# Moving weight decodes between the stages of a fused attention and two-mixer kernel

## The chip, the core and the metric

One core of a Trainium2 chip runs the whole program. The metric is the device time of one execution in microseconds (us); lower is better. The kernel before has a median of 1039.64 us over three runs (1037.52 to 1042.57). Engines: TensorE (PE in the profile; PEld is its weight load), VectorE (DVE), ScalarE (ACT), GpSimd (POOL) and the DMA queue of SyncE (SP).

## What is computed

```python
# q, k, v: 4 x 8 heads x 576 tokens x 64, float32; w_phi: 64 x 128
phi(x): proj = x @ w_phi;  proj -= max(|proj|);  concat(exp(proj), exp(-proj))
kv  = phi(k)^T @ v;  z = sum over tokens of phi(k)
x   = (phi(q) @ kv) / (phi(q) . z + 1e-6)          # then 4 x 576 x 512
u   = x + (x^T @ U @ V)^T                           # first mixer, rank 32
x   = u + relu(u @ w_ch1) @ w_ch2                   # 512 -> 2048 -> 512
u   = x + (relu(x^T @ w_tok1) @ w_tok2)^T           # second mixer, 576 -> 256 -> 576
out = u + relu(u @ w_ch1') @ w_ch2'                 # 512 -> 1536 -> 512
```

## The kernel before

**Number format.** The weights of the mixers arrive as float64. `decode64` (lines 161 to 176) turns a block of 128 x 512 of them into float32: two ACT conversions, `w` from the upper words (L166) and `r` from the lower words (L167), then two DVE bit operations, `r_` (L169) and `w_` (L172). Nearly every matmul is done in pieces: a number is split into a high part (a cast, L102 on ACT or L104 on DVE) and a low part (source minus high part, L107, on POOL or DVE), and three products replace one. `load_half` decodes and splits one **half**: of a tile of 128 hidden units, half 0 holds the first-layer weights (512 x 128) and half 1 the second-layer weights. Names follow: `w_a`, `wh_a`, `wl_a` are the decoded, high and low halves of stage A; `_b` and `_c` are stages B and C. The stage pool has two buffers for the raw words, two for `w`, two for `r`.

**Stage A.** The attention runs in rounds, five to each of 16 head pairs; `at(r, fn)` puts work into round r. In each round one `proj` makes features on PE (`pp`), takes the absolute maximum on DVE (`km`, L310) and subtracts it (`kd`, L107); `k1`, `k2`, `k3`, `q1`, `q2` exponentiate on ACT and multiply on PE (`kvp`, `dT`, `kvt`, `nm`). From the seventh head pair on (`NF32 = 6`), the features are split too (`keh`, `kel`, `qeh`, `qel`, KL), on ACT, DVE and POOL. The first mixer's channel layer has 16 hidden tiles; the first six (`NA`) are computed within the rounds, batch by batch (`ma_u`, `ma_h` for the hidden tile, `ma_y` for the second layer). `M_AT` starts this for batch 0 at round 37. The table `AT_WA` tells in which rounds the twelve halves of these six tiles are decoded (six first layers, then six second layers), and each is fetched `L_WA = 2` rounds before. High parts of first layers are cast on ACT, those of second layers on DVE, low parts are made on POOL.

**The end of stage A.** While batch 3 is computed, each `ma_h` calls `half_next`, which finishes the half that was decoded before (`parts`, `put_half`) and decodes the next one of the ten remaining tiles, which form five pairs. Four pairs have a place in SBUF (`wp`); the fifth gets one only when the attention's memory is given back. `AB.close()` ends the stage.

**Stages B and C.** `channel` computes a chunk of tokens: for each pair p of hidden tiles, `one(p)` (short chunks) or `seven(p)` (long chunks, seven products in place of eight) makes the hidden values (`hpb`, `hhb`, `hlb`), and `second` of the pair before adds to `yb`. Stage B has chunks of 256, 256, 512, 512, 512, 256 tokens, numbered 0 to 5. After each pair the chunk calls its **hooks**, lists of functions. From chunk 3 on, each chunk also carries the token mixing of one batch (`tokmix2`: `x2p`, `hhx`, `gp`, `m2p`) at its tail, and the last one is in chunk 0 of stage C. Weights of stage C have 24 halves. Those of pairs 0, 1, 2 and 5 are decoded by hooks of stage B (`decode`) and stored as float32 in DRAM (`wD`), fetched back late (`fetch_c`) and split (`weights_c`). Pairs 3 and 4 (`DIRECT`) are decoded and split in place (`direct`): one group of two halves in B chunk 5, three in C chunk 0.

**Order of the work.** A scheduler places each engine's instructions in one queue when the program is built, from the order of the code and its own estimates; on the chip each queue runs in that order. `tc.issue_after` keeps an instruction behind a given one.

```python
def ma_h(b, ch, f):                                  # L546
    a, v = relu_split(hp[:, :N], hh, hl)
    if b == B - 1:
        with tc.issue_after(a), tc.issue_after(v):
            for _ in range(2 if f == 0 else 1):
                half_next()
```

Of the kernel before, what the change touches and what calls it, by code (L numbers as in the profile page):

```python
# [8 lines left out]
F32 = mybir.dt.float32  # L9
# [10 lines left out]
P = 128  # L20
# [5 lines left out]
C = 512  # L26
# [7 lines left out]
NB = (NF1 - NA) // 2  # L34
NCP = NF2 // 2
# [60 lines left out]
def body(ctx, tc, kq, vd, w_phi, U, V, wm1, wt1, wt2, wm2, out):  # L96
    nc = tc.nc
# [41 lines left out]
    wD = [dr.tile([P, 2 * C], F32, name=f"wD{f}") for f in range(NF2)]  # L139
# [5 lines left out]
    stage = ctx.enter_context(tc.tile_pool(name="stage", bufs=RAWB))  # L145
# [52 lines left out]
    def h_tile(pool, w, uh, ul, name, tag="m"):  # L198
        hp = pool.tile([P, 512], F32, tag=tag, name=f"hp_{name}")
        wh, wl = w  # L200
        g = []
        for c in range(NC):
            g += [(w1(wh, c), uh[:, c, :]), (w1(wh, c), ul[:, c, :]), (w1(wl, c), uh[:, c, :])]
        group(hp[:, : uh.shape[2]], g)
        return hp

    def relu_split(hp, hh, hl):
        a = nc.scalar.activation(hh, hp, AF.Relu)  # L208
        v = nc.vector.scalar_tensor_tensor(out=hl, in0=hp, scalar=0.0, in1=f32(hh), op0=ALU.max, op1=ALU.subtract)  # L209
        return a.ins, v.ins  # L210
# [15 lines left out]
    wp = psm.tile([P, 512], F32, tag="m", name="wp")  # L226
# [43 lines left out]
    def at(r, fn, *args):  # L270
        rounds.setdefault(r, []).append((fn, args))
# [275 lines left out]
    def ma_h(b, ch, f):  # L547
        nm = f"a{b}_{ch}_{f}"
        hp = h_tile(psm, wA[f], *uhl[b, ch], nm)
        hh, hl = h_pair(f, nm)  # L550
        a, v = relu_split(hp[:, :N], hh, hl)
        if f < NA - 1 or b == B - 2:
            gates[:] = a, v
        hss[b, ch].append((hh, hl))
        if f == 3 and b < B - 2:
            ma_v(b, ch)
        if b == B - 1:
            with tc.issue_after(a), tc.issue_after(v):
                for _ in range(2 if f == 0 else 1):
                    half_next()  # L560

    def ma_s(b, ch, f):
        if f == 0:
# [130 lines left out]
    wp = {}  # L694
# [25 lines left out]
    def parts():  # L720
        while later:
            put_half(*later.pop(0))

    def half_next():
        parts()
        if not halves or halves[0][0] not in wp:
            return
        p, k, i = halves.pop(0)
        if p not in wB:
            wB[p] = pair_tiles(p, "b")  # L730
        later.append((firsts.pop(0) if firsts else take(), wB[p], k, i, "p"))
# [4 lines left out]
    for r in sorted(rounds):  # L736
        if r > end + 7:
            for fn, args in rounds[r]:
                fn(*args)
    while halves and halves[0][0] in wp:  # L740
        half_next()
    parts()
    PS.close()
    AB.close()
    psh = ctx.enter_context(tc.tile_pool(name="psh", bufs=2, space=PSUM, reuse_waits="tile"))
# [2 lines left out]
    pt = ctx.enter_context(tc.tile_pool(name="pt", **right))  # L748
# [2 lines left out]
    TX = ExitStack()  # L751
    tx = TX.enter_context(tc.tile_pool(name="tx", **right))

    words = [(f, k) for p in range(NCP) if p not in DIRECT for k in range(2) for f in (2 * p, 2 * p + 1)]

    def word(f, k):
        return wm2[f][:, k * C : (k + 1) * C], C, f"c{f}_{k}"
# [1 line left out]
    t1s = [(wt1[:, t], 256, f"t1_{t}") for t in range(NT)]  # L759
    t2s = [(wt2[:, j, k * N : (k + 1) * N], N, f"t2_{j}_{k}") for j in range(2) for k in range(2)]  # L760
    ts, ws = t1s + t2s, [word(*x) for x in words]
    stream += ts[:8] + ws[:1] + ts[8:] + ws[1:] + [word(2 * p + i, k) for p in DIRECT for k in range(2) for i in range(2)]

    def decode():
        f, k = words.pop(0)
# [2 lines left out]
    wC = {}  # L768
# [261 lines left out]
    def sums_b(p):  # L1030
        return lambda: sums(p, wB[p])

    def sums_c(p):
        return lambda: sums(p, wC[p])

    ahead = {}

    def fetch_c(p):
        ts = [stage.tile([P, 512], F32, tag=t, name=f"w_c{p}{n}", bufs=2) for n, t in enumerate("wwrr" * (p == 1))]
        for t in (3, 4) * (p != 1):  # L1040
            w = pt.tile([P, 2 * C], F32, tag=f"t{t}", name=f"w_c{p}t{t}")
            ts += [w[:, :C], w[:, C:]]
        ahead[p] = ts
        for n, w in enumerate(ts):
            nc.sync.dma_start(w, wD[2 * p + n % 2][:, n // 2 * C : (n // 2 + 1) * C])

    def weights_c(p):
        wC[p] = pair_tiles(p, "c")
        for n, w in enumerate(ahead.pop(p)):
            put_half(w, wC[p], n // 2, n % 2, "pv"[n % 2])  # L1050

    def direct(p, k):
        if p not in wC:
            wC[p] = pair_tiles(p, "c")
        for i in range(2):
            put_half(take(), wC[p], k, i, "v")
# [12 lines left out]
    def wc_of(p):  # L1069
        return lambda: weights_c(p)  # L1070

    d1, d2 = [decode], [decode, decode]

    def fc(p):
        return lambda: fetch_c(p)

    def dc(p, k):
        return lambda: direct(p, k)

    hooksB = [  # L1080
        {0: [half_next], 1: [half_next], 2: [half_next, sums_b(0)], 3: [half_next, sums_b(1)], 4: [parts]},
        {0: [sums_b(2)], 3: [sums_b(3)]},
        {0: [sums_b(4)] + tt[:1], 1: tt[1:3], 2: tt[3:6], 3: tt[6:8] + d1, 4: tt[8:] + d2},
        {0: d1, 1: d1, 2: d2, 3: d1, 4: d1},
        {0: d1, 1: d1, 2: d2, 3: d1, 4: d1},
        {0: d1 + [fc(0)], 1: [wc_of(0), fc(1)], 2: [wc_of(1), fc(2)], 3: [wc_of(2), dc(3, 0)]},
    ]
    for i, sl in enumerate(spans(CHUNKS_B)):
        if i >= 3:
# [5 lines left out]
    def last_mix():  # L1095
# [73 lines left out]
```

## Time and profile before

| | us |
|---|---|
| median of three runs | 1039.64 |
| lowest, highest | 1037.52, 1042.57 |
| profiled execution, device time | 1043.61 |
| its span on the core | 1041.8 |
| PE busy | 1004.4 (96%) |
| DVE busy | 686.2 (66%) |
| ACT busy | 450.6 (43%) |
| POOL busy | 198.8 (19%) |
| mean granted clock of TensorE | 0.993 |

The profiled execution took 1.8 us more than its span, and 3.97 us more than the median. A busy PE is not a PE at its peak: at a granted clock below 1 a matmul takes longer and still counts as busy. In timelines a number in brackets is the idle time of the engine just before the row, with what ended it.

### The profile page before, as it was taken

Reading aid. Unit: us, or ns where it says so; the run is one execution under the profiler, and the core shown is the slowest. Engines: PE = TensorE matmul, PEld = TensorE weight load, DVE = VectorE, ACT = ScalarE, POOL = GpSimd, SP = SyncE. Lnnn points to the kernel's source line nnn. Section 1 sums busy time; section 2 is a strip of 40 time slices with the busy share of each in tenths; the row PEclk is TensorE's granted clock in tenths of the full one; section 3 lists DMA queues with packets and bytes.
Section 4 is the critical chain, followed back from the end, with each engine's and each line's share of the span. In section 5 each row is a group of like instructions: output and inputs, shape, how many; then the busy total and the mean of one; then the engine's idle time right before and its main releaser. Section 6 shows DMA issues by size and latency. Waiting matters only on the chain. (4 is left out here: it accounts for less than half of the span.)

```text
span 1041.8 us, 17091 instructions
## 1 busy us (share of the span) xinstructions
PE 1004.4 (96%) x6586; PEld 919.5 (88%) x6586; DVE 686.2 (66%) x1279; ACT 450.6 (43%) x1058; POOL 198.8 (19%) x164
## 2 busy tenths in 40 slices
PE   9999888999999999899999999999999999999998
PEld 7777877999999998899989898898798898989897
DVE  6666997788678467778785754656678663544533
ACT  5666663556455346643453422333533221312211
POOL 2001576455544214310110000021010000000000
PEclk9999998999999999999999999999999999999999
DMA  7442531333321326622446363565412030120201
GB/s 216 122 116 87 165 130 51 95 96 101 91 61 58 108 70 202 209 90 60 135 149 227 117 212 105 177 208 181 154 46 102 1 121 2 41 81 1 82 1 41
DMA packets 77841, 112.31 MB, mean 108 GB/s; under 512 B 17984, under 2 KB 48960, under 8 KB 77760
## 3 DMA queue, kind: packets, MB, share of 16 engines
q1 hardware_dynamic: 77760, 111.22, 33.4%
q8 instruction: 52, 0.85, 0.3%
q14 instruction: 29, 0.24, 0.1%
HBM read 83.26 MB, written 27.86 MB: 107 GB/s over the span
## 5 line engine op out<-in xcount | busy, mean ns | idle before, releaser
L116 PE MATMUL yc<-hlc,vh_c 128*128 128x512 f32 (+1 forms) x240 | 88.1, 372 | 0.0
L116 PE MATMUL yc<-hhc,vl_c 128*128 128x512 f32 (+1 forms) x240 | 88.1, 372 | 0.0
L116 PE MATMUL pp<-KW,kq 128*128 128x256 f32 x320 | 83.4, 387 | 3.1 <-issue 2.2
L116 PE MATMUL yb<-hlb,vh_b 128*128 128x256 f32 (+1 forms) x240 | 80.3, 340 | 0.2 <-DVE hlb L209 0.2
L116 PE MATMUL yb<-hhb,vl_b 128*128 128x256 f32 (+1 forms) x240 | 79.5, 339 | 0.0
L116 PE MATMUL yc<-hhc,vh_c 128*128 128x512 f32 (+1 forms) x240 | 79.2, 372 | 0.0
L116 PE MATMUL yb<-hhb,vh_b 128*128 128x256 f32 (+1 forms) x240 | 68.7, 339 | 3.0 <-ACT hhb L208 3.0
L310 DVE TENSOR_REDUCE km<-pp 128x4 f32<-128x512 f32 x80 | 54.8, 685 | 21.5 <-PE pp L116 21.0
L116 PEld LDWEIGHTS pp<-KW,kq 128*128 128x128 f32 x320 | 58.0, 194 | 10.6 <-issue 3.3
L107 POOL TENSOR_TENSOR qel<-qe,qeh 128x640 fp32r<-128x640 f32 (+1 forms) x40 | 59.6, 1496 | 29.7 <-DVE qeh L104 20.8
L319 ACT ACTIVATE ke<-kd 128x256 f32<-128x256 f32 x80 | 33.2, 416 | 68.0 <-DVE kd L107 65.0
L116 PE MATMUL hp_a<-uha,wh_a 128*128 128x288 f32 x192 | 57.6, 301 | 4.7 <-DVE hla L209 4.7
L116 PE MATMUL yp<-hha,wh_a 128*128 128x288 f32 x192 | 58.5, 309 | 3.2 <-DVE hla L209 1.3
L116 PE MATMUL yp<-hha,wl_a 128*128 128x288 f32 x192 | 56.8, 302 | 1.5 <-POOL wl_a L107 1.5
L116 PE MATMUL hp_a<-ula,wh_a 128*128 128x288 f32 x192 | 57.2, 298 | 0.4 <-DVE ula L107 0.4
L116 PE MATMUL hp_a<-uha,wl_a 128*128 128x288 f32 x192 | 57.5, 300 | 0.0
L107 DVE TENSOR_TENSOR kd<-pp,km 128x512 f32<-128x512 f32 x80 | 54.8, 687 | 2.1
L116 PE MATMUL yp<-hla,wh_a 128*128 128x288 f32 x192 | 54.0, 301 | 0.2
L116 PEld LDWEIGHTS yc<-hhc,vl_c 128*128 128x128 f32 x240 | 45.1, 188 | 7.3
L107 POOL TENSOR_TENSOR kel<-ke,keh 128x512 fp32r<-128x512 f32 x30 | 41.2, 1380 | 51.6 <-ACT keh L102 51.1
L116 PEld LDWEIGHTS yc<-hlc,vh_c 128*128 128x128 f32 x240 | 45.3, 189 | 6.3
L116 PEld LDWEIGHTS yb<-hlb,vh_b 128*128 128x128 f32 x240 | 45.5, 190 | 5.1 <-DVE hlb L209 0.4
(336 smaller groups left out, 3034.2 us busy)
## 6 DMA issues: line engine op xcount, KB each, us to landing
raw_c<-in_wm_dram SPq DMA_DIRECT2D x24, 512.0 KB, 4.2
kq<-in_kq_dram SPq DMA_DIRECT2D x80, 128.0 KB, 2.7
raw_b<-in_wm_dram SPq DMA_DIRECT2D x20, 512.0 KB, 4.5
raw_a<-in_wm_dram SPq DMA_DIRECT2D x12, 512.0 KB, 3.9
rec<-rD SPq DMA_DIRECT2D x32, 144.0 KB, 3.2
u1D<-xT SPq DMA_DIRECT2D x8, 576.0 KB, 4.1
s1D<-ys SPq DMA_DIRECT2D x8, 576.0 KB, 3.9
x<-x2D SPq DMA_DIRECT2D x4, 1152.0 KB, 5.8
```

Of the source, the lines that this page charges most:

```text
L107: return ENG[e].tensor_tensor(out=o, in0=a, in1=b, op=ALU.subtract)
L116: m = nc.tensor.matmul(o, l, r, start=start, stop=stop, skip_group_check=True)
L310: nc.vector.tensor_reduce(out=m, in_=pv, op=ALU.max, axis=AX.X, apply_absolute_value=True)
L319: exps.append(nc.scalar.activation(e[:, :, 0, :], d, AF.Exp).ins)
```

## The change

Three things change; no arithmetic is added or left out.

1. `AT_WA` gets new rounds. The six first layers move from 7, 11, 16, 21, 25, 30 to 7, 10, 12, 15, 17, 20, the six second layers from 34, 36, 37, 39, 40, 42 to 22, 25, 29, 32, 36, 40.
2. `ma_h` of batch 3 decodes one half a call, also where it decoded two (f = 0 of both token halves). So two halves fewer are decoded in stage A, and the loop that finished the rest before `AB.close()` goes. Chunk 0 of stage B now decodes six halves: two in each of hooks 0 and 1, one in hooks 2 and 3. Before it decoded four, one in each.
3. The first layers of stage C's pair 3 are no longer decoded in place in B chunk 5. They are decoded by hooks 3 of B chunks 3 and 4 (one half more in each), stored as float32, fetched back in hook 2 of B chunk 5 and split in hook 0 of C chunk 0. The other three groups of two halves of pairs 3 and 4 come in hooks 0, 1 and 2 of C chunk 0 (before: two groups in hook 0 and one in hook 1).

```diff
-AT_WA = (7, 11, 16, 21, 25, 30, 34, 36, 37, 39, 40, 42)
-DIRECT = (3, 4)
+AT_WA = (7, 10, 12, 15, 17, 20, 22, 25, 29, 32, 36, 40)
+CW = ((0, 0), (0, 1), (1, 0), (1, 1), (2, 0), (2, 1), (5, 0), (5, 1), (3, 0))
+CD = ((3, 1), (4, 0), (4, 1))
...
-                for _ in range(2 if f == 0 else 1):
-                    half_next()
+                half_next()
...
-    while halves and halves[0][0] in wp:
-        half_next()
-    parts()
...
-    words = [(f, k) for p in range(NCP) if p not in DIRECT for k in range(2) for f in (2 * p, 2 * p + 1)]
+    words = [(2 * p + i, k) for p, k in CW for i in range(2)]
...
-    def fetch_c(p):
...
+    def fetch_c(p, ks=(0, 1), home="34"):
+        ts = []
+        for t in home:
+            if t in "wr":
+                ts += [stage.tile([P, 512], F32, tag=t, name=f"w_c{p}{t}{n}", bufs=2) for n in range(2)]
+            else:
+                w = pt.tile([P, 2 * C], F32, tag=f"t{t}", name=f"w_c{p}t{t}")
+                ts += [w[:, :C], w[:, C:]]
+        ahead[p] = [(w, ks[n // 2], n % 2) for n, w in enumerate(ts)]
+        for w, k, i in ahead[p]:
+            nc.sync.dma_start(w, wD[2 * p + i][:, k * C : (k + 1) * C])
...
     hooksB = [
-        {0: [half_next], 1: [half_next], 2: [half_next, sums_b(0)], 3: [half_next, sums_b(1)], 4: [parts]},
+        {0: [half_next] * 2, 1: [half_next] * 2, 2: [half_next, sums_b(0)], 3: [half_next, sums_b(1)], 4: [parts]},
...
-        {0: d1, 1: d1, 2: d2, 3: d1, 4: d1},
-        {0: d1, 1: d1, 2: d2, 3: d1, 4: d1},
-        {0: d1 + [fc(0)], 1: [wc_of(0), fc(1)], 2: [wc_of(1), fc(2)], 3: [wc_of(2), dc(3, 0)]},
+        {0: d1, 1: d1, 2: d2, 3: d2, 4: d1},
+        {0: d1, 1: d1, 2: d2, 3: d2, 4: d1},
+        {0: d1 + [fc(0)], 1: [wc_of(0), fc(1, (0, 1), "wr")], 2: [wc_of(1), fc(2), fc(3, (0,), "w")], 3: [wc_of(2)]},
...
-        {0: [dc(3, 1), dc(4, 0)], 1: [dc(4, 1)], 2: [sums_c(0)], 3: [wc_of(NB)], 5: [sums_c(1)], "flush": last_mix},
+        {0: [wc_of(3), dc(3, 1)], 1: [dc(4, 0)], 2: [dc(4, 1), sums_c(0)], 3: [wc_of(NB)], 5: [sums_c(1)], "flush": last_mix},
```

The order in the queues shows the moves. Up to line 558 the changed file's line numbers are higher by one than those of the file before.

The DVE queue while batch 0's hidden tiles are computed. `km` and `kd` belong to `proj`, `hla` is the low part of a hidden tile, `r_a`, `w_a` and `wh_a` are a half's decode and cast. Before:

```order
L169 SCALAR_TENSOR_TENSOR r_a_1_1459<-w_a_1_1458,r_a_1_1459 128x512
L310 TENSOR_REDUCE km_3_1475<-pp_3_1472 128x4
L209 SCALAR_TENSOR_TENSOR hla_0_4_1797<-hp_a_0_4_1783,hha_0_4_1796 128x288
L172 SCALAR_TENSOR_TENSOR w_a_1_1458<-w_a_1_1458,r_a_1_1459 128x512
L310 TENSOR_REDUCE km_4_1531<-pp_4_1528 128x4
L107 TENSOR_TENSOR kd_3_1477<-pp_3_1472,km_3_1475 128x512
L104 CAST keh_4_1538<-ke_4_1535 128x512
L104 CAST wh_a_624<-w_a_1_1458 128x512
L107 TENSOR_TENSOR kd_4_1533<-pp_4_1528,km_4_1531 128x512
L169 SCALAR_TENSOR_TENSOR r_a_1_1576<-w_a_1_1575,r_a_1_1576 128x512
L439 TENSOR_SCALAR pk_1525<-pk_1525 128x9
L209 SCALAR_TENSOR_TENSOR hla_0_5_1848<-hp_a_0_5_1834,hha_0_5_1847 128x288
```

The same place after the change:

```order
L108 TENSOR_TENSOR kd_2_1470<-pp_2_1465,km_2_1468 128x512
L311 TENSOR_REDUCE km_3_1493<-pp_3_1490 128x4
L108 TENSOR_TENSOR kd_3_1495<-pp_3_1490,km_3_1493 128x512
L105 CAST keh_4_1556<-ke_4_1553 128x512
L311 TENSOR_REDUCE km_4_1549<-pp_4_1546 128x4
L108 TENSOR_TENSOR kd_4_1551<-pp_4_1546,km_4_1549 128x512
L440 TENSOR_SCALAR pk_1543<-pk_1543 128x9
L210 SCALAR_TENSOR_TENSOR hla_0_3_1739<-hp_a_0_3_1725,hha_0_3_1738 128x288
L441 RECIPROCAL pk_1543<-pk_1543 128x9
L105 CAST qeh_0_0_1578<-qe_0_0_1575 128x640
L105 CAST qeh_1_0_1589<-qe_1_0_1586 128x640
L210 SCALAR_TENSOR_TENSOR hla_0_4_1797<-hp_a_0_4_1783,hha_0_4_1796 128x288
```

The decode operations that stood between the pieces of the attention are gone from here. From the first split of the mixer's input (`ula`) to the first sum of its output (`ys`), the DVE queue holds five halves and two of the three operations of a sixth before the change, and two halves after it; a third half's operations stand 5 to 14 rows ahead of `ula`.

The ACT queue where stage A ends and stage B begins. `hhb` is the first hidden value of B chunk 0, `vh_b` a cast of a decoded second-layer half. Before:

```order
L208 ACTIVATE hha_1_5_5302<-hp_a_1_5_5289 128x288
L166 ACTIVATE w_b_1_5269<-raw_b_1_5191 128x512
L102 CAST sh_b_5181<-w_b_0_5228 128x256 x2
L167 ACTIVATE r_b_1_5309<-raw_b_1_5234 128x512
L102 CAST vh_b_5183<-w_b_1_5269 128x512
L166 ACTIVATE w_b_1_5308<-raw_b_1_5234 128x512
L102 CAST vh_b_5183<-w_b_1_5308 128x512
L208 ACTIVATE hhb_0_0_5411<-hpb_0_0_5398 128x256
L208 ACTIVATE hhb_0_1_5428<-hpb_0_1_5415 128x256
```

After:

```order
L209 ACTIVATE hha_1_5_5280<-hp_a_1_5_5267 128x288
L168 ACTIVATE r_b_0_5287<-raw_b_0_5210 128x512
L167 ACTIVATE w_b_0_5286<-raw_b_0_5210 128x512
L103 CAST sh_b_5243<-w_b_0_5247 128x512
L209 ACTIVATE hhb_0_0_5387<-hpb_0_0_5374 128x256
L209 ACTIVATE hhb_0_1_5404<-hpb_0_1_5391 128x256
L103 CAST sh_b_5243<-w_b_0_5286 128x256 x2
L167 ACTIVATE w_b_1_5412<-raw_b_1_5253 128x512
L168 ACTIVATE r_b_1_5413<-raw_b_1_5253 128x512
L168 ACTIVATE r_b_1_5423<-raw_b_1_5292 128x512
L167 ACTIVATE w_b_1_5422<-raw_b_1_5292 128x512
L209 ACTIVATE hhb_1_0_5443<-hpb_1_0_5430 128x256
```

Two halves' conversions and casts moved from ahead of the first two `hhb` to behind them.

The DVE queue at the end of B chunk 5, before its last pair's hidden values `hlb_4`. Before:

```order
L107 TENSOR_TENSOR sl_c_8413<-w_c2t_8348,sh_c_8412 128x256 x2
L169 SCALAR_TENSOR_TENSOR r_c_0_8431<-w_c_0_8430,r_c_0_8431 128x512
L172 SCALAR_TENSOR_TENSOR w_c_0_8430<-w_c_0_8430,r_c_0_8431 128x512
L169 SCALAR_TENSOR_TENSOR r_c_0_8441<-w_c_0_8440,r_c_0_8441 128x512
L107 TENSOR_TENSOR u2c_8720<-uc_8717,u1c_8719 128x1024
L172 SCALAR_TENSOR_TENSOR w_c_0_8440<-w_c_0_8440,r_c_0_8441 128x512
L107 TENSOR_TENSOR vl_c_8415<-w_c2t_8349,vh_c_8414 128x512
L209 SCALAR_TENSOR_TENSOR hlb_4_0_8490<-hpb_4_0_8476,hhb_4_0_8489 128x256
L107 TENSOR_TENSOR sl_c_8427<-w_c_0_8430,sh_c_8426 128x512
L209 SCALAR_TENSOR_TENSOR hlb_4_1_8507<-hpb_4_1_8493,hhb_4_1_8506 128x256
```

After:

```order
L108 TENSOR_TENSOR sl_c_8435<-w_c2t_8366,sh_c_8434 128x256 x2
L108 TENSOR_TENSOR u2c_8716<-uc_8713,u1c_8715 128x1024
L108 TENSOR_TENSOR vl_c_8437<-w_c2t_8367,vh_c_8436 128x512
L210 SCALAR_TENSOR_TENSOR hlb_4_0_8486<-hpb_4_0_8472,hhb_4_0_8485 128x256
L210 SCALAR_TENSOR_TENSOR hlb_4_1_8503<-hpb_4_1_8489,hhb_4_1_8502 128x256
```

Four decode operations and one subtraction are gone from ahead of `hlb_4_1`.

## Rows read from the trace of the kernel before

**Rows 1.** The page's first part: busy time, share of the span and instructions of each engine.

```profile
PE 1004.4 (96%) x6586; PEld 919.5 (88%) x6586; DVE 686.2 (66%) x1279; ACT 450.6 (43%) x1058; POOL 198.8 (19%) x164
```

**Rows 2.** Windows, all engines: busy us (instructions), granted clock, DMA share, GB/s.

```profile
19.00:105.00 86.00, 81.56 (x396) 65.68 (x396) 59.48 (x103) 59.23 (x159) 9.50 (x9) 1.00 0.43 119
105.00:177.00 72.00, 60.15 (x366) 53.71 (x365) 64.61 (x96) 42.51 (x105) 48.24 (x35) 0.93 0.38 118
177.00:345.00 168.00, 166.48 (x1202) 161.52 (x1201) 130.10 (x215) 94.68 (x245) 87.94 (x68) 1.00 0.28 86
425.00:440.00 15.00, 11.39 (x76) 10.75 (x75) 11.51 (x18) 7.75 (x16) 5.97 (x5) 0.89 0.79 254
440.00:465.00 25.00, 25.00 (x214) 25.00 (x213) 15.26 (x31) 11.88 (x26) 5.33 (x5) 1.00 0.27 86
560.00:700.00 140.00, 139.11 (x893) 125.61 (x892) 79.53 (x153) 45.44 (x93) 5.32 (x4) 1.00 0.49 166
```

**Rows 3.** Waits of PE in 105 to 177: total us, times, longest.

```profile
PE hp_a L116 <- DVE hla L209: 2.0, 2, 1.7
PE dT L396 <- DVE kd L107: 2.0, 1, 2.0
PE yp L116 <- POOL wl_a L107: 1.5, 3, 0.7
PE kvp L116 <- DVE kel L107: 1.3, 1, 1.3
PE kvp L116 <- POOL kel L107: 1.2, 1, 1.2
```

**Rows 4.** Windows of tile w_a alone: DVE, ACT, POOL, then clock and DMA.

```profile
19.00:105.00 86.00, 8.60 (x12) 7.84 (x12) 6.52 (x6) 1.00 0.43 119
105.00:177.00 72.00, 15.88 (x18) 3.99 (x6) 9.42 (x7) 0.93 0.38 118
```

**Rows 5.** Timeline of DVE (start, us): decode operations of stage A at two places.

```profile
66.25 0.68 DVE L169 SCALAR_TENSOR_TENSOR r_a<-w_a,r_a 128x512 int32<-128x512 int32 x1
139.80 0.41 DVE L104 CAST wh_a<-w_a 128x512 fp32r<-128x512 f32 x1
140.74 1.16 DVE L169 SCALAR_TENSOR_TENSOR r_a<-w_a,r_a 128x512 int32<-128x512 int32 x1
```

**Rows 6.** Timelines of DVE and PE around 65: the longest wait of 19 to 105.

```profile
62.20 0.17 DVE L439 TENSOR_SCALAR pk<-pk 128x9 f32<-128x9 f32 x1 [2.49 <-DMA pk<-nd]
...
65.11 1.10 PE L116 MATMUL pp<-KW,kq 128*128 128x256 f32 x4 [2.00 <-issue]
```

**Rows 7.** Timelines of PE, ACT and DVE where B chunk 0 begins.

```profile
431.86 0.28 PE L116 MATMUL hpb<-u5b,sl_b 128*128 128x256 f32 x1
435.14 0.96 PE L116 MATMUL yb<-hhb,vh_b 128*128 128x256 f32 x4 [3.00 <-ACT hhb L208]
...
434.18 0.62 ACT L102 CAST vh_b<-w_b 128x512 fp32r<-128x512 f32 x1 [2.09 <-DVE w_b L172]
...
430.71 1.54 DVE L574 TENSOR_TENSOR ys<-yp,xT 128x288 f32<-128x288 f32 x4
```

**Rows 8.** Timelines of PE, DVE and ACT, end of B chunk 5 and C chunk 0.

```profile
702.60 0.38 PE L116 MATMUL hpb<-u5b,sh_b 128*128 128x256 f32 x1 [0.30 <-DVE hlb L209]
710.66 0.66 PE L989 MATMUL x2p<-ident,x 128*128 128x128 f32 x4 [1.64 <-DVE hlb L209]
743.38 0.73 PE L116 MATMUL gp<-hhx,T1H 128*128 128x512 f32 x2 [1.15 <-ACT hhx L386]
...
704.76 0.68 DVE L169 SCALAR_TENSOR_TENSOR r_c<-w_c,r_c 128x512 int32<-128x512 int32 x1
707.88 1.80 DVE L172 SCALAR_TENSOR_TENSOR w_c<-w_c,r_c 128x512 int32<-128x512 int32 x1
710.20 0.41 DVE L209 SCALAR_TENSOR_TENSOR hlb<-hpb,hhb 128x256 fp32r<-128x256 f32 x1
...
741.65 0.66 ACT L166 ACTIVATE w_c<-raw_c 128x512 f32<-128x512 f32 x1 [3.62 <-DMA raw_c<-in_wm_dram]
```

More of the change, by code (lines that the diff above doesn't have):

```diff
@@ L761, in body @@
     ts, ws = t1s + t2s, [word(*x) for x in words]
-    stream += ts[:8] + ws[:1] + ts[8:] + ws[1:] + [word(2 * p + i, k) for p in DIRECT for k in range(2) for i in range(2)]
+    stream += ts[:8] + ws[:1] + ts[8:] + ws[1:] + [word(2 * p + i, k) for p, k in CD for i in range(2)]
     def decode():
@@ L1036, in body @@
     ahead = {}
-    def fetch_c(p):
[L1039 to L1045, printed above, removed]
+    def fetch_c(p, ks=(0, 1), home="34"):
[9 more added lines that the diff above has]
+            nc.sync.dma_start(w, wD[2 * p + i][:, k * C : (k + 1) * C])
     def weights_c(p):
         wC[p] = pair_tiles(p, "c")
-        for n, w in enumerate(ahead.pop(p)):
-            put_half(w, wC[p], n // 2, n % 2, "pv"[n % 2])
+        for w, k, i in ahead.pop(p):
+            put_half(w, wC[p], k, i, "pv"[i])
     def direct(p, k):
@@ L1072, in body, with fc @@
     d1, d2 = [decode], [decode, decode]
-    def fc(p):
-        return lambda: fetch_c(p)
+    def fc(p, *where):
+        return lambda: fetch_c(p, *where)
     def dc(p, k):
```

## The prediction

> **What bounds the kernel now.** Start with the page's first part [rows 1]: PE is busy 96% of the span, so no change of order can win more than PE's idle time, 1041.8 - 1004.4 = 37 us, and what it loses at a lower clock. The next question is where those losses lie, and windows by stretch answer it [rows 2]. In 177 to 345 PE is busy 166.48 of 168 us at full clock: nothing to win. In 105 to 177, where the attention's splits and the first mixer's hidden tiles overlap and six halves are decoded, PE is idle 72 - 60.15 = 11.85 us. The granted clock there is 0.93: part of it ran at 1.2 instead of 2.4 GHz, which costs PE (1 - 0.93) x 72 = 5.0 us more. DVE is busy 64.61 of 72 us there, against 130.10 of 168 in the next stretch. So this stretch is bound by DVE and by POOL's splits, not by PE. The waits say the same [rows 3]: PE waits for low parts from DVE (`hla`, `kel`) and POOL (`kel`, `wl_a`) and for `kd`; only `wl_a` is a decode product, the others queue behind decodes. A second loss is at 425 to 440 [rows 2]: 3.6 us idle and clock 0.89, (1 - 0.89) x 15 = 1.65 us. One wait makes most of it [rows 7]: `yb` waits 3.00 us for the first `hhb`, and ACT, which should make it, stands 2.09 us at a `vh_b` cast that waits for a decode on DVE. A third is at 700 to 711 [rows 8].
>
> **19 to 105: three more decodes.** By the DVE queue, six halves of stage A are decoded before about 105 now, nine after the change. Those added are second layers: two DVE bit operations and a DVE cast each. With POOL idle a bit operation takes 0.68 us and the cast 0.41 [rows 5]. That is 1.77 us of DVE a half, 5.3 us in all, on a DVE that is busy 59.48 of 86 us and a POOL busy 9.50 [rows 2]. The cover is PE's own 81.56 us. If it goes, all 5.3 us lie on the path; the other bound is zero. PE idles 86 - 81.56 = 4.4 us there, with nine decodes (six of stage A, three of the mixing weights), so I take 0.5 us for each of three: **+1.5**. Raw fetches also stand in SP's queue ahead of small transfers. The longest wait there is of that kind [rows 6]: DVE sat 2.49 us at `pk` for a DMA, and PE then 2.00 us; this is within the bound.
>
> **105 to 177: three fewer.** Six halves keep DVE 15.88 us here, against 8.60 for the twelve bit operations of 19 to 105 [rows 4]: here they are slower, since POOL works beside them (1.16 against 0.68 for the same operation [rows 5]). Half of them go: 7.9 us of DVE, and with three of the seven `wl_a` 4.0 of POOL's 9.42. The lower bound of the gain is the waits that a decode makes directly, 1.5 for `wl_a` and 1.7 for the longest `hla`: 3.2. The upper bound: DVE's remaining 64.6 - 7.9 = 56.7 us must still be done, so at most 72 - 56.7 = 15.3; PE at full clock needs 60.15 - 5.0 = 55.1. Between them I let the idle time halve with the halves, 5.9 us, and the clock give back three fifths of its 5.0, 3.1, as the waits it follows thin out: **-9.0**.
>
> The row on `r_a` bears a price: moving one bit operation away from POOL makes it 0.48 us shorter [rows 5]. The Trainium skill (SBUF — State Buffer, on the engine ports) says that VectorE and GpSimd share one port pair as an exclusive lock, and that an operation with two SBUF inputs then waits until a reading GpSimd instruction ends. The rule would count not only DVE's busy time but also POOL's waiting: by it the three halves would free 7.9 + 4.0 = 11.9 us, an estimate, and the gain would be near the upper end. By the rows alone POOL's part does not lie on DVE's queue, and the waits for `kd` and `hla` are on DVE, so I stay with the sum above.
>
> **The end of stage A.** In the new ACT queue both `vh_b` casts and the last two decodes stand behind the first two `hhb`. The 3.00 us wait [rows 7] then goes. What is late next is `hlb` on DVE: it stands behind four `ys` sums, which end at 430.71 + 1.54 = 432.25, and takes 0.4 us, while PE has work until 431.86 + 0.28 = 432.14. So 0.5 us stays and 2.5 go, and with them the 1.65 of the clock. Against this, hooks 0 and 1 of B chunk 0 hold four decodes where there were two. There PE is busy 25.00 of 25, DVE 15.26, ACT 11.88 [rows 2], so two more halves fit; but `hhb` of pair 2 now stands behind two raw transfers. That costs between nothing and another 3.0; I take 0.5, near the idle ACT. Together 2.5 + 1.65 - 0.5 = 3.65: **-3.6**.
>
> **Stages B and C.** One decode more in each of B chunks 3 and 4, two float32 blocks stored and fetched: PE is busy 139.11 of 140 us in 560 to 700, DVE 79.53, DMA 0.49 [rows 2]. Cost **0**, hidden by PE; without that cover two halves' bit operations, 4 x 0.7 = 2.8. At 700 to 711, decodes stand ahead of `hlb`, the second bit operation alone 1.80 us [rows 8]; they leave the queue, and the waits of 0.30 and 1.64 with them: **-1.9**, and no less than -0.5 if the splits of pair 2, which stay, hold `hlb` up. The wait of 1.15 in C chunk 0 stays: ACT stands 3.62 us at a raw transfer ahead of `hhx`, and hook 1 still brings one.
>
> **The sum.** 1.5 - 9.0 - 3.6 + 0 - 1.9 = -13.0. From the profiled execution's 1043.61 that gives 1030.6. The median is 3.97 lower. Three runs spread over 5 us and the profiled one lies above all of them, so some of its waits or its slow clock will be missing in a median run; I therefore do not take all of the gain off the median, but 11 of 13: 1039.64 - 11 = **1028.6 us**. A change within 0.5%, 5.2 us, is about what a measurement of this kernel can't tell from none.
>
> **Rivals.**
> - *The stretch 105 to 177 stays bound by the splits.* POOL's `kel` and DVE's `kd` and `kel` make 1.2 + 2.0 + 1.3 of the waits [rows 3] and none is a decode. If they only move, the stretch gives the 3.2 of the direct waits and the clock nothing: 1.5 - 3.2 - 3.6 - 1.9 = -7.2 on the profiled execution, about -5 on the median: 1034.6; with pair 2 of B chunk 0 late by 2 us more, 1036.6. For it: POOL is busy 48.24 of 72 [rows 2] and keeps nine tenths of that. Against it: in 177 to 345 the same splits go on, no half is decoded, and PE is full.
> - *The early attention becomes the bound: slower.* The place is 19 to 105. There the added conversions on ACT (59.23 of 86 busy) and bit operations on DVE (59.48) stand in the queues between `km`, `kd` and the exponentials, each `pp` buffer is late, and the clock falls there as it does in 105 to 177. Price: three halves at 2 x 0.66 on ACT (7.84 for twelve [rows 4]) and 1.8 on DVE in line, 9.3, plus a clock loss as large as that of the next stretch, 5.0, plus up to two waits like that of rows 6 for a late transfer, 4.0: 18.3. With only the 3.2 of the direct waits and the lower bounds of the other two places won, 2.5 + 1.65 - 3.0 = 1.15 and 0.5, that is 18.3 - 4.85 = +13.5 on the profiled execution, and about 11 on the median: 1051. It decides from about 10 us on, that is, only if ACT and DVE both fill. For it: PE already waits there for `pk` and DVE. Against it: 5.3 us more on DVE leave it 21 us idle. The Trainium skill (TensorE: Matmul & The Clock Gate, on the second failure mode) says that many tiny idles between groups of matmuls can make the clock fall too. By that rule this rival gains; the trace does not bear it out for this stretch, where 4.4 us of idle left the clock at 1.00 [rows 2].
> - *All of it goes.* The waits of 105 to 177 vanish with the decodes and the clock stays full: -15.3 there, 1.5 - 15.3 - 3.6 - 1.9 = -19.3, some -17 on the median: 1022.6.
>
> **How the numbers follow.** My sum has 0.56, the first rival 0.20, the slow one 0.09, the large gain 0.15. The range of 1020 to 1038 holds the sum with its bounds, the large gain and most of the first rival; it leaves out the slow one and the tails. Faster by over 0.5% means below 1034.4: my sum's chance and the large gain's, and a fifth of the first rival's: 0.75. Slower by over 0.5% is the slow rival without its mild half, 0.08. The rest is 0.17.
>
> **What would show it.** Right: in the new trace the stretch from the first `hp_a` to the end of the slow clock has DVE busy clearly below 90% and PE's waits for `wl_a` gone; no wait near 3 us at the first `yb`; no wait for `hlb` before the last token mixing of stage B. Wrong: waits for `kel`, `qel` or `kd` as long as before in that stretch, a clock below 1 in the first 105 us, or a wait for `hhb` in pairs 2 and 3 of B chunk 0.

## The result and the profile after

| | before | after |
|---|---|---|
| median, us | 1039.37 (4 runs) | 1028.82 (4 runs) |
| lowest, highest | 1037.52, 1042.57 | 1027.92, 1029.76 |
| profiled execution, its span | 1043.61, 1041.8 | 1027.92, 1026.1 |
| mean granted clock | 0.993 | 0.998 |

The ratio is 0.9895, with a 95% interval of 0.9869 to 0.9922: faster by 1.05%. The time is that of the forecast (1028.6), but the terms that make it up are not; the experiments sort them. The profiled execution of after is the fastest of its four, and that of before lies above all of its own, so the two profiles differ by more (15.7 us) than the medians (10.6).

The first part of the page of after answers to [rows 1]. PE's idle time is 27.2 us where it was 37.4, and 5.5 us of busy time went with the slow clock.

```profile
PE 998.9 (97%) x6586; PEld 915.9 (89%) x6586; DVE 673.0 (66%) x1278; ACT 449.3 (44%) x1058; POOL 202.5 (20%) x165
```

The windows of after, in the order of [rows 2] (PE, PEld, DVE, ACT, POOL, granted clock, DMA share, GB/s). The work now comes earlier, so the same stretch of time holds some later work.

```profile
19.00:105.00 86.00, 82.45 (x400) 66.59 (x399) 64.45 (x113) 64.36 (x171) 14.39 (x12) 1.00 0.48 138
105.00:177.00 72.00, 67.60 (x474) 64.19 (x474) 61.22 (x97) 41.97 (x111) 44.65 (x34) 1.00 0.38 116
177.00:345.00 168.00, 165.23 (x1191) 159.71 (x1190) 120.56 (x210) 91.83 (x236) 89.69 (x67) 1.00 0.25 76
425.00:440.00 15.00, 14.73 (x122) 14.32 (x122) 12.91 (x22) 9.32 (x21) 4.49 (x5) 1.00 0.30 88
440.00:465.00 25.00, 24.63 (x206) 24.24 (x206) 21.90 (x55) 9.65 (x23) 1.29 (x1) 1.00 0.30 95
560.00:700.00 140.00, 137.06 (x898) 123.73 (x897) 81.66 (x151) 49.35 (x101) 8.73 (x6) 1.00 0.53 174
```

In 105 to 177 PE is busy 67.60 us and not 60.15, at clock 1.00 and not 0.93, and runs 474 matmuls where it ran 366. In 19 to 105 DVE and ACT have 5 us more work each, and PE lost nothing.

The waits of PE in 105 to 177 of after, for [rows 3], and the windows of tile `w_a` alone (DVE, ACT, POOL), for [rows 4]:

```profile
PE hp_a L117 <- DVE hla L210: 1.3, 2, 1.1
PE pp L117 <- issue: 1.2, 1, 1.2
PE dT L397 <- DVE kd L108: 1.0, 2, 0.7
PE hp_a L117 <- DVE ula L108: 0.9, 1, 0.9
```

```profile
19.00:105.00 86.00, 13.58 (x21) 10.41 (x16) 11.45 (x9) 1.00 0.48 138
105.00:177.00 72.00, 8.15 (x9) 1.32 (x2) 4.00 (x3) 1.00 0.38 116
```

The waits for `wl_a` and for both `kel` are gone, those for `kd` and `hla` shorter. The decodes' share of DVE in 105 to 177 fell by 7.7 us and POOL's by 5.4, close to the 7.9 and 4.0 of the forecast.

To see where the end moved, take the first and last start of a tile on its engine. First, count with min/median/max duration in ns, then the two starts in us. Before:

```profile
L116 PE MATMUL hpb<-u5b,sh_b x70: 277/283/415, 429.1 to 704.5; 128*128 128x256 f32 x70
L102 ACT COPY eb<-xb x15: 350/372/377, 492.2 to 651.7; 128x256 f32<-128x256 f32 x15
L116 PE MATMUL hpc<-u1c,sh_c x48: 277/282/294, 729.3 to 779.1; 128*128 128x256 f32 x48
L116 PE MATMUL xc<-t0c,sh_c x96: 277/280/384, 782.0 to 1022.3; 128*128 128x256 f32 x96
```

After:

```profile
L117 PE MATMUL hpb<-u5b,sh_b x70: 277/283/391, 412.5 to 688.1; 128*128 128x256 f32 x70
L103 ACT COPY eb<-xb x15: 345/372/374, 472.5 to 635.1; 128x256 f32<-128x256 f32 x15
L117 PE MATMUL hpc<-u1c,sh_c x48: 277/281/387, 711.6 to 763.2; 128*128 128x256 f32 x48
L117 PE MATMUL xc<-t0c,sh_c x96: 277/281/384, 766.0 to 1006.9; 128*128 128x256 f32 x96
```

Stage B (first `hpb`) starts 16.6 us earlier. B chunk 2 (first `eb`) starts 19.7 earlier: chunks 0 and 1 took 60.0 us, not 63.1. Then time is given back: from first `eb` to first `hpc` 239.1 us, not 237.1, and chunk 0 of stage C (first `hpc` to first `xc`) 54.4, not 52.7. The rest took 0.3 us more. The sum is -16.6 - 3.1 + 2.0 + 1.7 + 0.3 = -15.7, the difference of the spans.

The place of the loss is in the timelines of PE and ACT of after around C chunk 0, against [rows 8]:

```profile
691.64 0.66 PE L986 MATMUL x2p<-ident,x 128*128 128x128 f32 x4 [0.31 <-DVE hlb L210]
726.52 0.98 PE L117 MATMUL gp<-hhx,T1H 128*128 128x512 f32 x2 [2.36 <-ACT hhx L387]
...
724.79 0.66 ACT L168 ACTIVATE r_c<-raw_c 128x512 int32<-128x512 uint32 x1 [3.31 <-DMA raw_c<-in_wm_dram]
```

The wait of `x2p` for `hlb` is 0.31 us where it was 1.64, as forecast. But `gp` waits 2.36 us for `hhx` where it waited 1.15, since ACT stands 3.31 us at a raw transfer ahead of that cast. The granted clock of 720 to 730 is 0.84.

### The profile page after: what moved, and what is told of

The parts are those of the page before. It is cut to its first block, busy times and chain, and to the rows that moved or that the text cites. A ratio compares the mean times of both kernels' runs of the same rounds, so it can differ in the third digit from the quotient of the medians.

```text
span 1026.1 us, 17093 instructions
## 1 busy us (share of the span) xinstructions
PE 998.9 (97%) x6586; PEld 915.9 (89%) x6586; DVE 673.0 (66%) x1278; ACT 449.3 (44%) x1058; POOL 202.5 (20%) x165
## 4 chain that ended last, share of the span: by engine, by line
PE 78%; DVE 9%; DMA 5%; ACT 4%; issue 2%; SPq 0%; POOL 0%; DVEq 0%; ACTq 0%
PE yc L117 15%; PE yb L117 10%; PE pp L117 6%; PE hp_a L117 5%; PE yp L117 5%; PE kvp L117 5%; PE nm L117 5%; PE vc L117 3%; PE zc L117 3%; PE xc L117 3%; PE m2p L117 3%; PE gp L117 2%; DMA raw_b<-in_wm_dram 2%; PE vb L117 2%; PE xb L117 2%
```

## The experiments

The theory on the main term: the decodes in 105 to 177 held the attention up through the in-order DVE queue, so fewer of them there is what pays. Its rivals: POOL and the sharing of DVE's time with it, the early attention as a new bound, and a larger share for the parts at the end of stage A. All runs of before in these batches have medians of 1039.6 to 1040.5.

### Each part alone

**The rounds alone** (kernel before with one line changed):

```diff
-AT_WA = (7, 11, 16, 21, 25, 30, 34, 36, 37, 39, 40, 42)
+AT_WA = (7, 10, 12, 15, 17, 20, 22, 25, 29, 32, 36, 40)
```

> The kernel before with the new decode rounds of stage A alone. My theory (decodes crowd DVE in 105 to 177): it carries most of the gain, 8 to 12 us, so 1028 to 1031; the granted clock stays at 1.00 there, and the 3.00 us wait for the first hhb of stage B stays. Rival (the splits bound that stretch, the gain comes from the end of stage A): 3 us or less, 1036 or more, with the slow clock still there.

Measured: 1030.86 us (1030.23 to 1032.3), ratio 0.9917 [0.9901, 0.9934]: -9.3 on the medians. The wait of 3.0 us for the first `hhb` stays, as expected, and 105 to 177 is at full clock:

```profile
105.00:177.00 72.00, 66.69 (x468) 62.95 (x467) 61.76 (x96) 40.67 (x107) 43.75 (x33) 1.00 0.38 115
```

**The end of stage A alone**:

```diff
-                for _ in range(2 if f == 0 else 1):
-                    half_next()
+                half_next()
...
-    while halves and halves[0][0] in wp:
-        half_next()
-    parts()
...
-        {0: [half_next], 1: [half_next], 2: [half_next, sums_b(0)], 3: [half_next, sums_b(1)], 4: [parts]},
+        {0: [half_next] * 2, 1: [half_next] * 2, 2: [half_next, sums_b(0)], 3: [half_next, sums_b(1)], 4: [parts]},
```

> The kernel before with only the two halves moved from stage A to chunk 0 of stage B. My theory: 3 to 6 us less, 1033 to 1036: the 3.00 us wait for hhb and the slow clock behind it go, chunk 0 pays 0.5 or less for the two more decodes. Rival (the wait moves to pairs 1 to 3 of chunk 0): within 1 us of the kernel before.

Measured: 1034.56 us (1032.3 to 1035.38), ratio 0.9945 [0.9927, 0.9962]: -5.6. The 3.00 us wait is gone; 0.3 us of waits for `hhb` is left in the whole trace.

**Pair 3 alone** (the changed kernel with both other parts undone):

```diff
-AT_WA = (7, 10, 12, 15, 17, 20, 22, 25, 29, 32, 36, 40)
+AT_WA = (7, 11, 16, 21, 25, 30, 34, 36, 37, 39, 40, 42)
...
-                half_next()
+                for _ in range(2 if f == 0 else 1):
+                    half_next()
...
+    while halves and halves[0][0] in wp:
+        half_next()
+    parts()
...
-        {0: [half_next] * 2, 1: [half_next] * 2, 2: [half_next, sums_b(0)], 3: [half_next, sums_b(1)], 4: [parts]},
+        {0: [half_next], 1: [half_next], 2: [half_next, sums_b(0)], 3: [half_next, sums_b(1)], 4: [parts]},
```

> The kernel before with only the first layers of stage C's pair 3 kept as float32 in DRAM. The prediction's step: 1.9 us less, 1037.5. The trace of the changed kernel speaks for the contrary: 2 to 4 us more, 1041 to 1043, since the wait for hhx in C chunk 0 is 2.36 us instead of 1.15 and the clock falls behind it, and B chunks 3 and 4 wait 0.9 us for ACT's copy e.

Measured: 1040.55 us, ratio 1.0008 [0.9992, 1.0025]: no difference, so neither expectation came true. This run tells something else too. Its stage A is that of the kernel before, and its row for 105 to 177 is

```profile
105.00:177.00 72.00, 61.08 (x395) 55.43 (x394) 67.14 (x98) 43.66 (x107) 50.61 (x37) 0.98 0.40 121
```

with a clock of 0.98, not 0.93. So of the 5.0 us that the clock cost there in the profiled execution of before, (0.98 - 0.93) x 72 = 3.6 belong to that one execution, and a usual one loses 1.4 (0.98 is the clock in the profiles of all four other runs with this stretch's old rounds).

**The first two parts together, without pair 3** (the edits of the first two diffs):

> The changed kernel without its third part. If the third part costs time, this is 2 to 4 us faster than the changed kernel's 1028.8: 1025 to 1027. If the prediction's step on it was right, it is 1.9 us slower: 1030.7.

Measured: 1026.71 us (1024.27 to 1027.74), ratio 0.9869 [0.9852, 0.9887]: -13.5, near the sum of -9.3 and -5.6. Pair 3 brings nothing to these two.

What the end of stage A gave was in part not where the forecast had it. The windows of the kernel before show idle time of PE there that nothing in the forecast priced:

```profile
390.00:405.00 15.00, 14.36 (x107) 13.90 (x106) 9.27 (x14) 9.77 (x21) 6.16 (x6) 1.00 0.64 205
405.00:415.00 10.00, 8.07 (x53) 7.07 (x54) 9.01 (x14) 5.89 (x11) 4.07 (x3) 1.00 0.66 208
```

With the end of stage A alone changed, the same two windows are full:

```profile
390.00:405.00 15.00, 15.00 (x114) 14.88 (x113) 11.04 (x16) 9.41 (x19) 7.19 (x6) 1.00 0.62 204
405.00:415.00 10.00, 10.00 (x77) 10.00 (x76) 5.40 (x12) 6.20 (x14) 4.49 (x4) 1.00 0.56 168
```

From the first `hp_a` to the first `hpb` that run took 307.4 us, the run with pair 3 alone 310.1: 2.7 less, and chunks 0 and 1 of stage B 59.5 us against 64.1 there and 63.1 before. Part of both differences is clock: in the run of pair 3 alone it was 0.83 in 405 to 415 and 0.77 in 425 to 440. The idle time that went in 390 to 415 is 0.64 + 1.93 = 2.6 us by the rows above.

### DVE's queue or POOL's

**High parts of second layers on ACT** (kernel before; this takes the casts of second layers off DVE):

```diff
-WHI = {"a": "av", "b": "aa", "c": "av"}
+WHI = {"a": "aa", "b": "aa", "c": "av"}
```

> The kernel before, with the high parts of stage A's second-layer halves cast on ACT in place of DVE; nothing is moved in time. It takes 4.3 of the 15.9 us that the six decodes keep DVE in 105 to 177, and puts them on ACT, which is busy 42.5 of 72. If DVE's queue is what the stretch is bound by: 3 to 5 us less, 1035 to 1036.5. If POOL's splits bind it: within 1 us of 1039.4.

Measured: 1036.8 us (1035.12 to 1039.55), ratio 0.9962 [0.9947, 0.9976]: -3.7. Taking six casts off DVE's queue alone buys 3.7 us, although ACT and POOL got no less to do. All engines, 105 to 177; at the same clock of 0.98, PE is busy 2.5 us more than in the run of pair 3 alone:

```profile
105.00:177.00 72.00, 63.60 (x414) 57.98 (x413) 61.75 (x95) 47.30 (x115) 49.44 (x37) 0.98 0.39 123
```

**Low parts of second layers on DVE** (kernel before; work moves from POOL to DVE):

```diff
-WLO = {"a": "pp", "b": "pp", "c": "pv"}
+WLO = {"a": "pv", "b": "pp", "c": "pv"}
```

> The kernel before, with the low parts of the odd stage A halves (the second layers) made on DVE in place of POOL: 6 x 0.68 = 4.1 us more on DVE and 6 x 1.3 = 8 less on POOL in 105 to 177. If DVE's queue binds the stretch: 2 to 5 us more, 1041 to 1044. If POOL binds it: 3 to 6 us less, 1033 to 1036.

Measured: 1038.27 us (1035.58 to 1039.93), ratio 0.998 [0.9965, 0.9995]. Neither expectation of a clear change came true. The reason is in DVE's groups of 105 to 177 (busy us, mean ns of one, idle before). Kernel before:

```profile
L107 DVE TENSOR_TENSOR kd<-pp,km 128x512 f32<-128x512 f32 x15 | 10.2, 684 | 0.2
L107 DVE TENSOR_TENSOR kel<-ke,keh 128x512 fp32r<-128x512 f32 x3 | 4.0, 1341 | 0.0
L107 DVE TENSOR_TENSOR ula<-xT,uha 128x1152 fp32r<-128x1152 f32 x2 | 3.6, 1818 | 0.0
```

This kernel:

```profile
L107 DVE TENSOR_TENSOR kd<-pp,km 128x512 f32<-128x512 f32 x15 | 10.1, 682 | 0.1
L107 DVE TENSOR_TENSOR wl_a<-w_a,wh_a 128x512 fp32r<-128x512 f32 x6 | 5.4, 899 | 0.0
L107 DVE TENSOR_TENSOR kel<-ke,keh 128x512 fp32r<-128x512 f32 x3 | 3.1, 1018 | 0.0
L107 DVE TENSOR_TENSOR ula<-xT,uha 128x1152 fp32r<-128x1152 f32 x2 | 2.7, 1344 | 0.0
```

DVE got 5.4 us of `wl_a`, and its busy time is 64.88 us where it was 64.61. DVE's own `kel` takes 1018 ns, not 1341, and `ula` 1344, not 1818; `kd` stays at 684. What decides is not how busy POOL is in the stretch, which is 48.24 us in the kernel before and 39.65 here: in the changed kernel `ula` takes 1952 ns with POOL busy 44.65. It is whether a POOL operation runs at that moment. The mean of 1818 hides two durations, 1.34 and 2.29 us; the longer one began while POOL made a `wl_a` (in the changed kernel the longer one, 2.56 us, began beside a `qel`). Kernel before, then this kernel, where POOL's next operation starts at 123.95:

```profile
121.63 1.29 POOL L107 TENSOR_TENSOR wl_a<-w_a,wh_a 128x512 fp32r<-128x512 f32 x1 [0.36 <-DVE wh_a L104]
121.84 2.29 DVE L107 TENSOR_TENSOR ula<-xT,uha 128x1152 fp32r<-128x1152 f32 x1
...
122.72 1.35 DVE L107 TENSOR_TENSOR ula<-xT,uha 128x1152 fp32r<-128x1152 f32 x1
```

So DVE's time in this stretch is in part POOL's. The Trainium skill (SBUF — State Buffer, on the engine ports) says that the two engines share one port pair as a lock; the rows agree with that. But moving the low parts won nothing beyond 0.2%: DVE's busy time stayed the same, and PE's waits for `wl_a` (1.5 us before) are now 2.3 us, on DVE. By these rows both loads count in this stretch, and a decode weighs on both; a run that lightens POOL without loading DVE was not made.

### More decodes early

**All twelve halves in rounds 7 to 29** (the changed kernel otherwise):

```diff
-AT_WA = (7, 10, 12, 15, 17, 20, 22, 25, 29, 32, 36, 40)
+AT_WA = (7, 9, 11, 13, 15, 17, 19, 21, 23, 25, 27, 29)
```

> The changed kernel with all twelve halves of stage A decoded in rounds 7 to 29, every second round, so that none is left beside the first mixer and twelve lie in 19 to 105. My theory: the overlap loses its last two or three decodes and the waits that go with them, up to 3 us, and the early stretch, where DVE is 64.5 and ACT 64.4 of 86 us busy now, pays 0 to 2: 1027 to 1029. Rival (the early attention becomes the bound): 3 us or more above 1028.8, with new waits of PE for kd or pp before 105.

Measured: 1021.54 us (1018.39 to 1025.03), ratio 0.9819 [0.9785, 0.9852], some 7 us below the changed kernel.

```profile
19.00:105.00 86.00, 80.34 (x386) 63.90 (x385) 68.91 (x119) 65.75 (x171) 18.51 (x15) 1.00 0.55 153
105.00:177.00 72.00, 71.62 (x508) 68.83 (x507) 56.16 (x92) 40.85 (x109) 40.13 (x32) 1.00 0.32 98
```

With no decode left in 105 to 177, PE is full there (71.62 of 72). The price in 19 to 105 is 82.45 - 80.34 = 2.1 us of PE for three more halves, with the clock at 1.00. That is the upper end: over all profiles PE is busy 80.79 to 82.45 us there with nine halves early (five) and 79.98 to 80.47 with twelve (three), 1.5 us less by the middle ones. The rival in which the early attention becomes the bound is refuted: even twelve halves do not make it one.

### Pair 3 and the wait for `hhx`

**Two groups of decodes moved away from that wait** (the changed kernel):

```diff
-        {0: [wc_of(3), dc(3, 1)], 1: [dc(4, 0)], 2: [dc(4, 1), sums_c(0)], 3: [wc_of(NB)], 5: [sums_c(1)], "flush": last_mix},
+        {0: [wc_of(3), dc(3, 1)], 2: [dc(4, 0), sums_c(0)], 3: [dc(4, 1), wc_of(NB)], 5: [sums_c(1)], "flush": last_mix},
```

> The changed kernel with the last four direct halves of C chunk 0 taken one hook later (hooks 2 and 3 in place of 1 and 2), so that no raw transfer stands ahead of hhx in ACT's queue. If the wait of 2.36 us for hhx and the clock of 0.84 behind it come from that transfer: 3 to 4 us less than the changed kernel, 1025 to 1026, with gp no longer waiting for hhx. If hhx is late for another cause, such as its own source on PE: no change.

Measured: 1028.3 us (1025.89 to 1028.87), ratio 0.9879 [0.9856, 0.9901], the same as the changed kernel. The wait of `gp` is gone, so the raw transfers ahead of `hhx` were its cause; but the gain expected with that did not come. Another wait took its place a little later, with DVE full. Waits of PE, then the window of all engines:

```profile
PE hpc L117 <- DVE hlc L210: 2.3, 1, 2.3
```

```profile
750.00:760.00 10.00, 7.20 (x58) 6.79 (x58) 10.00 (x18) 5.72 (x14) 3.15 (x2) 1.00 0.13 45
```

**Early rounds with and without pair 3, and the changed kernel again**, on one chip. The first is the kernel before with the first two parts and the early rounds above.

> The kernel before with the early rounds 7, 9, 11 to 29 for the halves and the new end of stage A, and without the third part (pair 3's first layers are still decoded in place). Theory A (the third part costs about 2 us whatever stands ahead of it, by its new wait for hhx in chunk 0 of stage C): about 2 us less than the same early rounds with the third part, so 1019.5 where that gives 1021.5, and waits x2p for hlb of 1.6 and gp for hhx of 1.2 in the trace as before. Theory B (the third part costs nothing; 1026.7 against 1028.8 was the spread of runs): the same as with it, within 1 us.

> The changed kernel with the early rounds 7, 9, 11 to 29, as run before (1021.5 us), now beside the version without the third part and the changed kernel itself on one chip. Both theories: 1020 to 1023. Theory A: 2 us above the version without the third part; theory B: equal to it within 1 us.

> The changed kernel itself once more on the chip of the two early versions. Both theories: 1027 to 1030, 6 to 8 us above the changed kernel with early rounds. If the gain of the early rounds was a run's luck, the two are closer than 4 us.

| | median, us | range | ratio to before |
|---|---|---|---|
| early rounds, without pair 3 | 1019.63 | 1018.76 to 1022.42 | 0.9813 [0.9794, 0.9831] |
| early rounds, with pair 3 | 1023.68 | 1021.48 to 1025.64 | 0.9844 [0.9826, 0.9863] |
| the changed kernel | 1026.31 | 1022.37 to 1028.52 | 0.9865 [0.9845, 0.9885] |

The version without pair 3 is the fastest kernel of the study, 20 us (1.9%) below before. Pair 3 costs 4.0 us on the medians here, more than either expectation, and the early rounds gain 2.6 with it in this batch (7.3 between batches). By the expectation set for it, a difference under 4 us means that part of the first gain of the early rounds was a run's luck; over all executions of both batches the medians are 1028.1 (ten of the changed kernel) and 1023.4 (nine with early rounds), a gain of 4.7. The expected traces of the version without pair 3 came true: `x2p` waits 1.4 us for `hlb` and `gp` 1.0 for `hhx`. Against the changed kernel's own rounds (1026.71 without pair 3, 1028.82 and 1026.31 with it) the cost of pair 3 is not told from none.

The same kernel, early rounds with pair 3, was profiled twice, and the two profiles show one way in which its cost varies. First the timeline (raw transfers on SP's queue, ACT's wait for them, PE's wait) and the window of all engines of the run in the section before:

```profile
715.87 9.41 SPq L155 DMA_DIRECT2D raw_c<-in_wm_dram  x4
721.61 0.67 ACT L168 ACTIVATE r_c<-raw_c 128x512 int32<-128x512 uint32 x1 [2.58 <-DMA raw_c<-in_wm_dram]
723.35 0.73 PE L117 MATMUL gp<-hhx,T1H 128*128 128x512 f32 x2 [1.34 <-ACT hhx L387]
```

```profile
720.00:730.00 10.00, 8.54 (x50) 6.97 (x51) 6.85 (x12) 6.19 (x12) 0.00 (x0) 1.00 0.51 182
```

Then the same of the run of this batch:

```profile
713.96 10.00 SPq L155 DMA_DIRECT2D raw_c<-in_wm_dram  x4
720.30 0.66 ACT L168 ACTIVATE r_c<-raw_c 128x512 int32<-128x512 uint32 x1 [3.18 <-DMA raw_c<-in_wm_dram]
722.04 0.74 PE L117 MATMUL gp<-hhx,T1H 128*128 128x512 f32 x2 [2.30 <-ACT hhx L387]
```

```profile
720.00:730.00 10.00, 7.84 (x33) 6.25 (x34) 6.90 (x12) 6.11 (x12) 0.00 (x0) 0.83 0.34 118
```

The transfers took 0.6 us longer, ACT and PE waited 0.6 and 1.0 us more, and then the clock of 720 to 730 was 0.83. C chunk 0 took 52.4 us in the first and 54.5 in the second, of which 1.4 is PE's busy time (50.7 us against 49.4) and 0.7 its idle time. Elsewhere the second profile won as much: the two spans are 1021.6 and 1021.9 us. In the run of pair 3 alone `gp` waited 1.0 us and the chunk took 52.3, no more than before.

Over all profiles this wait sorts the cost. From first `eb` to first `xc` the seven profiles without pair 3 took 289.4 to 290.7 us. The two with it whose `gp` waited 1.0 and 1.3 us took 290.1 and 290.8; the three whose `gp` waited 2.2 to 2.4 us, with a slow clock behind it, took 292.6 to 293.5. (The kernel with the decodes moved away is left out, since its `xc` starts in another place.)

The part up to the first `hpc`, B chunks 2 to 5, is longer by about 1 us in all of them: 236.7 to 237.8 us in the seven profiles without pair 3, 237.8 to 239.1 in the six with it. There are new waits of `xb` for `eb` on ACT (0.9 us in all), but the wait of `x2p` is 1.3 us shorter, and PE's idle time is the same (3.4 to 4.3 us without, 3.2 to 4.3 with). What grew is PE's busy time, at full clock: 233.3 to 233.8 us without, 234.6 to 234.9 with. The rows of before and of pair 3 alone:

```profile
492.20:729.30 237.10, 233.40 (x1512) 211.15 (x1512) 148.65 (x295) 88.98 (x193) 16.09 (x15) 1.00 0.51 169
488.10:725.90 237.80, 234.58 (x1512) 211.34 (x1511) 147.36 (x292) 87.80 (x190) 16.31 (x15) 1.00 0.52 173
```

## Why the prediction was right, and which steps were not

The total came out within 0.3 us, and that is luck: the errors cancelled. The first two parts gave 13.5 us together where the sum had 1.5 - 9.0 - 3.6 = -11.1 for them, and the third part gave nothing where it had -1.9.

1. **19 to 105, +1.5.** Not borne out, and small. PE's idle time went from 4.4 to 3.55 us in the two profiles; the other profiles with nine halves early have 3.6 to 5.2 and those with six have 4.1 to 5.3, so a cost is not told from none. The 5.0 us more of DVE's busy time (5.3 were forecast) lay under PE. The wait of 2.0 us for `issue` [rows 6] is not in the profile of after (two others with nine halves have one of 1.4 and 1.6); that a late transfer made it was a guess, since `issue` names nothing that released it. The runs with all twelve halves early show a price from the tenth half on, some 0.5 us each by the middle profiles, which is the price forecast for the seventh to ninth. The sentence of the Trainium skill (TensorE: Matmul & The Clock Gate, on the second failure mode) that many small idles bring the clock down found no support: 5.7 us of idle in 86 left it at 1.00. It was below 1.00 here in one profile only, 0.98 with the end of stage A alone, behind a single wait of 2.1 us.

2. **105 to 177, -9.0.** The mechanism is right: the rounds alone, which carry this term and the one above (-7.5 together), give -9.3 on the medians, and the signs named (DVE below 90%, no `wl_a`) are there. The first of them says little: DVE is at 85% of 105 to 177 after and was at 90% before. The two sizes inside were off. Idle time fell by 7.45 us (rule of halving: 5.9), and the clock gave back all of its 5.0 on the profiled execution, not 3.1; but 3.6 of these were that execution's own, so the medians show less than the profiles. DVE's busy time fell only from 64.61 to 61.22, not to 56.7, since the freed time took in work that came earlier: nine `hla` in place of six. That the upper bound of 15.3 was not reached, though the rule on the ports pointed to it, fits with six operations and three casts of decodes that are still there; with none, PE is full.

3. **The end of stage A, -3.6.** Right on its place: no wait near 3 us is left at the first `yb`, no `hhb` late in pairs 2 and 3 (0.7 us of waits for `hhb` in the whole kernel, 0.28 of them in B chunk 0). Too small in all: alone it gives -5.6, since the two halves that leave stage A also free 2.6 us of idle time in 390 to 415, which the forecast did not cost. The step that failed is the list of what moves, "2.5 + 1.65 - 0.5": it holds the longest wait and its clock, and nothing for the shorter waits ahead of it.

4. **Stages B and C, 0 and -1.9.** The wrong step. Of the two waits for `hlb` that were to go, that of `x2p` did (1.64 to 0.31), but that of `hpb` went from 0.30 to 0.75 in the profile of after. "The wait of 1.15 in C chunk 0 stays" failed: it became 2.36, with a slow clock behind it. "Cost 0, hidden by PE" failed too: B chunks 2 to 5 lost 2.0 between these two profiles, some 1 us over all of them, and mostly as PE's busy time, not as waits. Where -1.9 was forecast, the spans of these two executions show 2.0 + 1.7 = +3.7 from B chunk 2 to C chunk 0; on the medians pair 3 costs between nothing and 4.0 us. The cause of the longer wait is the order: the groups that were ahead in hooks 0 and 1 now come in hooks 0, 1 and 2, nearer to the token mixing, and each waits for a raw transfer on ACT ahead of `hhx`; with two groups taken behind it, the wait was gone.

5. **The sum.** -13.0 was forecast on the profiled execution and -15.7 came; 11 on the median and 10.6 came (13.2 in the second batch). Taking less off the median than off the profile was right, and the reason given (slow clock and waits of that one execution) is borne out: from first `hp_a` to first `hpb` it took 315.1 us, where the run of pair 3 alone, with the same stage A, took 310.1 (and the two runs with casts or low parts on another engine 308.9 and 309.5).

6. **The rivals.** The splits did not bind: the waits for `kel` vanished with the decodes. The early attention did not become the bound. The large gain, -19.3, was not had by this change, but the early rounds without pair 3 come to it (-19.9 on the medians, where some -17 was forecast for this rival).

Open: why the clock fell in some executions of before at 170 to 177 and not in others; why PE's busy time in B chunks 2 to 5 is 1.2 us longer with pair 3; and how much of the gain of the rounds is POOL's and not DVE's. No run settles these.

## What to carry to other kernels

Move work out of the stretch where the helper engines are full into one where the bound engine covers them, and go on until the bound engine shows a loss: here twelve halves early paid more than nine. Count every place a removed operation leaves, not only the one with the longest wait. When decodes fed by a transfer are moved in an in-order queue, look at what stands behind each: here 0.6 us more of a transfer went with 2.1 us more of a chunk.

## What the runs showed of the hardware

One wait of PE can cost more than itself. In the run of early rounds with pair 3, PE waits 2.10 us for `ys`, and matmuls of one shape change their pace shortly behind it:

```profile
336.01 0.40 PE L117 MATMUL yp<-hha,wh_a 128*128 128x288 f32 x1 [2.10 <-DVE ys L599]
336.24 0.30 PE L117 MATMUL yp<-hla,wh_a 128*128 128x288 f32 x1
336.38 0.30 PE L117 MATMUL yp<-hha,wl_a 128*128 128x288 f32 x1
...
337.41 0.44 PE L117 MATMUL yp<-hha,wl_a 128*128 128x288 f32 x1
337.65 0.44 PE L117 MATMUL yp<-hha,wh_a 128*128 128x288 f32 x1
```

The starts are 0.14 us apart first and 0.24 later, and the granted clock of 338 to 342 is 0.71: the lower of the two levels, 1.2 GHz, for a part of it. Five profiles have a wait of 2.1 us at this place: the clock fell behind it in four of them, with pair 3 or without (0.83 to 0.85 over 10 us, some 1.6 us lost), and not in the changed kernel's first. Where the wait was 1.4 or 1.5 us (three profiles) it stayed at 1.00. At `gp` the clock stayed at 1.00 behind waits of 1.0 to 1.4 us and fell behind those of 2.2 to 2.4; behind the 2.3 us at `hpc` above it stayed. At the first `yb` it fell behind waits of 2.8 to 3.2 us in all five profiles that have one (0.72 to 0.84 over 10 us). So the length of one wait does not settle it.

The second is the contention between DVE and POOL: the same DVE subtraction of two SBUF operands took 1.34 us with POOL idle, and 2.29 us where it began 0.2 us after a POOL subtraction of 1.29 us, while one that reads its source from the matmul's output (`kd`) stayed at a mean of 682 to 686 ns in every profile. A mean over both kinds of moment (1818 ns) hides this.
